# Attention with top-k, then GELU and two matrix products: PSUM banks that hold two sums are opened by their first real product, without a product of zeros

## The chip, the cores and the metric

The kernel runs on one core of a Trainium2 chip. A core has five engines with a program each: TensorE (PE) multiplies matrices, VectorE (DVE), ScalarE (ACT) and GpSimd (POOL) work element by element, SyncE (SP) issues DMA transfers. The engines run side by side and wait for each other by semaphores. TensorE writes its results to PSUM, a memory of 8 banks of 128 partitions by 512 numbers (float32), and other engines copy them from there to SBUF, the large memory on the core. The metric is the time of one execution on the device in microseconds (us), the median of several runs.

## The reference

```python
# q, k, v: 8 batches x 8 heads x 576 rows x 64
scores = scale * np.matmul(q, k.transpose(0, 1, 3, 2))
kth = np.partition(scores, -32, axis=-1)[..., -32:-31]
scores = np.where(scores >= kth, scores, -1000000000.0)
scores = scores - np.max(scores, axis=-1, keepdims=True)
attn = np.exp(scores)
attn = attn / (np.sum(attn, axis=-1, keepdims=True) + 1e-09)
x = np.matmul(attn, v)        # heads side by side: 4608 rows x 512
h = x @ w_in                  # 512 x 2048
g = 0.5 * h * (1.0 + erf(h * inv_sqrt2))
out = g @ w_out               # 2048 x 512
```

Everything is float32. In each row of scores the 32 largest are kept, the rest is left out of the softmax.

## The kernel before, in words

**Slots.** The order of the work on all engines is written out by hand. The main loop at the end of the kernel goes through the items of attention, 144 of them, each 128 query rows of a pair of heads. One pass of the loop is a slot, of 10 to 12 us. In slot `n` TensorE computes the scores of item n+2 (`scores`, L341 and L357, s_ps, and `last_keys`, L303, the last 64 keys), VectorE finds the 32 largest of each row of item n (`top_k`: MAX8 on L378, MATCH_REPLACE8 on L381, four and three times for each of two heads), ScalarE makes the softmax of item n-1 (`softmax`, L417 and L418), GpSimd scales it (`normalise`, L431) with reciprocals by VectorE (`inverse`, L404), TensorE transposes the weights of item n-2 (`transposes`, L455, L458, L481) and multiplies those of item n-3 with v (`attend`, L538 and L549).

**The two products behind attention** are cut into pieces that `mlp` sets between these steps, on TensorE's queue. The rows of x are taken in 20 ranges: 16 of 256 rows and 4 of 128. A `first_block` has the pieces of x @ w_in (`l1_piece`, L594, into h_ps); ScalarE's GELU (L610) makes g of it; a `second_block` has the pieces of g @ w_out. A range of 256 rows has four first and four second blocks, each for four of the 16 slices of 128 along the 2048 columns of g.

The second product has three forms:

- `full_piece` (L689), the very first range: one product of 512 columns after another into a bank.
- `even_piece` (L707, L710), the four ranges of 128 rows: even and odd slices are summed in the two halves of one bank, `acc[0]`; the other 256 columns in one half of a second bank, `acc[1]`.
- `seven_piece` and `trio_piece`, through `products` (L743, L745), the 15 other ranges: two by two blocks are multiplied with seven products in place of eight. The sums and differences of w_out (`weight_sums`) and of g (`sums`, L625 to L628) are made by GpSimd. Product 7 goes to a bank `seven` and from there to SBUF at once (L761, L764). The six others are paired into three banks, `TRIO = ((1, 2), (6, 5), (4, 3))`: each bank holds two sums of 256 columns, one a half, which grow over the four blocks of the range. At the end ScalarE copies them out (L786 to L803) and GpSimd puts them together (L795 to L810). For the last range VectorE does that (`last_parts`, L827 to L837).

**Banks.** The accumulating banks have the tags y0, y1 and y2, one buffer each. From a few slots after the weights are in, all other small results of TensorE take turns on one bank with the tag z (`bank`: t_ps, tp_t, o, tp_qk, seven), so that each waits until the one before has been copied out.

**How a bank with two sums is opened.** A product with `start=True` overwrites its place, one with `start=False` adds to it. `acc_tile` gives the tile of a bank, and with `open_bank` it first issues a product of zeros over all 512 columns (L668), flagged as the start. Its operands are read again and again from a single column `none` of zeros in bfloat16. All real products into the bank are then issued with `start=False`. Banks that take one sum (L689, L710, `seven`) are flagged on their first real product. `trio_piece` calls `acc_tile` in the first block of a range, for each of its three banks just ahead of the first product into it: the first bank follows `seven`, with the transposes of the slot (L303, L455 or L458, then eight of L481) between the first bank's products and those of the other two. `even_piece` calls it for the first slice.

Of the kernel before, what the change touches and what calls it, by code (L numbers as in the profile page):

```python
# [14 lines left out]
def kernel(  # L15
# [19 lines left out]
    nc = tc.nc  # L35
    f32, i32, u32 = mybir.dt.float32, mybir.dt.int32, mybir.dt.uint32
    bf16, i16, u16 = mybir.dt.bfloat16, mybir.dt.int16, mybir.dt.uint16
# [4 lines left out]
    P = 128  # L42
# [9 lines left out]
    FT = DFF // P  # L52
# [3 lines left out]
    HALF = DM // 2  # L56
# [5 lines left out]
    const = ctx.enter_context(tc.tile_pool(name="const", bufs=1))  # L62
    work = ctx.enter_context(tc.tile_pool(name="work", bufs=2))
    ps = ctx.enter_context(tc.tile_pool(name="ps", bufs=2, space=bass.MemoryType.PSUM))
# [506 lines left out]
    g_of, acc, h_of = {}, {}, {}  # L571
# [5 lines left out]
    B1, B2 = slice(0, HALF), slice(HALF, DM)  # L577
# [65 lines left out]
    def store(tok, y):  # L643

        lo = 0
        while lo < P:
            two, at = divmod(tok + lo, RING)
            b, row, end = (
                (0, at, SM + TL) if at < SM + TL
                else (1, at - TL, SM + 2 * TL) if at < SM + 2 * TL  # L650
                else (1, at - SM - 2 * TL, RING)
            )
            m = min(end - at, P - lo)
            row += (2 * two + b) * S
            nc.sync.dma_start(out=out[row : row + m, :], in_=y[lo : lo + m])
            lo += m

    none = const.tile([P, 1], bf16, name="none")
    nc.gpsimd.memset(none, 0.0)

    def zeros(n):
        return bass.AP(tensor=none.tensor, offset=none.offset, ap=[list(none.ap[0]), [0, n]])

    def acc_tile(x, open_bank=True):

        t = ps.tile([P, 2, HALF], f32, tag=f"y{x}", bufs=1, name="y_ps")
        if open_bank:
            nc.tensor.matmul(  # L668
                t.rearrange("p a n -> p (a n)"), lhsT=zeros(P), rhs=zeros(2 * HALF),
                start=True, stop=False,  # L670
            )
        return t

    def y_tile():
        return work.tile([P, DM], f32, tag="y", name="y")

    def part_tile():
        return work.tile([P, HALF], f32, tag="part", bufs=3, name="part")

    def full_piece(u, x):  # L680

        tok, n, f0, nf = units[u]
        i, sub = divmod(x, 2)
        f = f0 + i
        assert NWI + f // 2 in made
        if f == 0:
            acc[sub] = acc_tile(sub, False)
        g = g_of[u - u % 2][:, u % 2].rearrange("p (f n) -> p f n", f=nf)
        nc.tensor.matmul(  # L689
            acc[sub].rearrange("p a n -> p (a n)"), lhsT=g[:, i, sub * P : (sub + 1) * P],  # L690
            rhs=w_out_sb[:, f, :], start=(f == 0), stop=(f == FT - 1),
        )
        if f == FT - 1:
            y = y_tile()
            nc.scalar.copy(out=y, in_=acc.pop(sub).rearrange("p a n -> p (a n)"))
            store(tok + sub * P, y)

    def even_piece(u, f_at):

        tok, n, f0, nf = units[u]  # L700
        f = f0 + f_at
        assert f // 2 in summed
        if f == 0:
            acc[0], acc[1] = acc_tile(0), acc_tile(1, False)
        lhsT = g_of[u - u % 2][:, u % 2].rearrange("p (f n) -> p f n", f=nf)[:, f_at]
        w = w_out_sb[:, f]
        nc.tensor.matmul(  # L707
            acc[0][:, f % 2], lhsT=lhsT, rhs=w[:, B1], start=False, stop=(f == FT - 1)
        )
        nc.tensor.matmul(  # L710
            acc[1][:, 0], lhsT=lhsT, rhs=w[:, B2], start=(f == 0), stop=(f == FT - 1)
        )
        if f == FT - 1:
            y, e = y_tile(), part_tile()
            nc.scalar.copy(out=e, in_=acc[0][:, 0])
            nc.scalar.copy(out=y[:, B1], in_=acc[0][:, 1])
            nc.scalar.copy(out=y[:, B2], in_=acc[1][:, 0])

            def end():
                nc.gpsimd.tensor_tensor(y[:, B1], y[:, B1], e, op=ALU.add)  # L720
                nc.gpsimd.tensor_tensor(y[:, B2], y[:, B2], e, op=ALU.add)
                store(tok, y)

            small.append((2, end))

    def products(u, names, x):

        _, _, f0, _ = units[u + x]
        j = f0 // 2
        assert j in summed and NWI + j in made  # L730
        g = g_of[u][:, x].rearrange("p (f n) -> p f n", f=2)
        t = sums_of[u][:, x]
        e, o, w = w_out_sb[:, f0], w_out_sb[:, f0 + 1], w_sum[:, j]
        lo, hi = slice(0, P), slice(P, 2 * P)
        sides = {
            1: (g[:, 0, lo], e[:, B1]), 2: (g[:, 1, lo], o[:, B1]), 3: (t[:, 2], o[:, B2]),
            4: (g[:, 1, hi], w[:, 2]), 5: (t[:, 0], e[:, B2]), 6: (t[:, 1], w[:, 0]),
            7: (g[:, 0, hi], w[:, 1]),
        }
        for k, name in enumerate(names):  # L740
            lhsT, rhs = sides[name]
            if name == 7:
                nc.tensor.matmul(seven[0][:, 0:HALF], lhsT=lhsT, rhs=rhs, start=(x == 0), stop=(x == 1))  # L743
                continue
            nc.tensor.matmul(  # L745
                acc[names][:, k], lhsT=lhsT, rhs=rhs,
                start=False, stop=(j == FT // 2 - 1 and k == 1),
            )

    seven, small = [None], []  # L750
# [3 lines left out]
    def seven_piece(u):  # L754
        j = units[u][2] // 2
        seven[0] = bank("seven")
        for x in range(2):
            products(u, (7,), x)
        if j == 0:
            y7[0] = work.tile([P, HALF], f32, tag="y7", bufs=2, name="y7")  # L760
            nc.scalar.copy(out=y7[0], in_=seven[0][:, 0:HALF])  # L761
            return
        t = work.tile([P, HALF], f32, tag="p7", bufs=1, name="p7")
        nc.scalar.copy(out=t, in_=seven[0][:, 0:HALF])  # L764
        into = y7[0]
        small.insert(0, (1, lambda: nc.gpsimd.tensor_tensor(into, into, t, op=ALU.add)))
# [3 lines left out]
    def trio_piece(u, names, x):  # L770
        tok, _, f0, _ = units[u + x]
        j, k = f0 // 2, TRIO.index(names)
        if j == 0:
            acc[names] = acc_tile(k)
        products(u, names, x)
        if j < FT // 2 - 1:
            return
# [169 lines left out]
    for pair in range(2, n_pairs):  # L947
        b, p = divmod(pair, NP)
# [131 lines left out]
```

## Time and profile before

| | before |
|---|---|
| median of 3 runs | 1619.91 us (1619.59 to 1622.13) |
| the profiled execution | 1620.02 us |
| its span, first to last instruction | 1618.2 us |
| mean granted clock of TensorE | 0.997 |
| VectorE busy, 0 to 134 us | 126.4 us |
| TensorE / VectorE busy, 230 to 620 us | 385.7 / 357.2 us |
| TensorE / VectorE busy, 1530 to 1618 us | 81.6 / 7.2 us |
| bytes moved by DMA | 56.31 MB, 35 GB/s |

The profile is of one execution. PE stands for TensorE's products and PEld for the loads of their weights, which run beside the product before. A float32 product is two passes, with a row each for load and product; a bfloat16 product or a transpose is one pass. The end of a product is modelled and covers its whole passage, so that rows of consecutive products overlap: what a product costs is read from the start of one to the start of the next. The time of a row is counted from the span's start. In a row of the timeline, a bracket tells how long the engine was idle before it, and what ended that. The chain of waits is followed back from the last instruction, at each step to what released it or to the instruction before it on its engine; "issue" is time for which the profile shows no reason.

### The profile page before, as it was taken

The numbers are of one execution on the slowest core, as the hardware profiler recorded it, in microseconds if no ns is written. First come the engines' busy times: TensorE is split into PE (matmuls) and PEld (weight loads), VectorE is DVE, ScalarE is ACT, GpSimd is POOL, SyncE is SP. The second block draws the span as 40 slices with busy tenths as digits, with TensorE's granted clock in tenths as the row PEclk, the third lists the DMA queues.
The fourth block names the chain that finished last, engine by engine and source line by source line (L and its number), as shares of the span: only waits on it lengthen the run. The fifth ranks groups of instructions, "written<-read, shape, count | busy, mean of one in ns | idle before, by whom it ended". The sixth has DMA issues, their size and how long they took to land.

```text
span 1618.2 us, 27709 instructions
## 1 busy us (share of the span) xinstructions
PE 1578.8 (98%) x10062; PEld 1269.9 (78%) x10081; DVE 1415.7 (87%) x3052; ACT 1205.9 (75%) x2122; POOL 772.9 (48%) x1045
## 2 busy tenths in 40 slices
PE   7899999999999999999999999999999999999998
PEld 6776678888787778888787778888878777888887
DVE  8999989989999889998999898998999988999800
ACT  6989877777778777777777777777777877776730
POOL 4775766433544445433454535443454444543442
PEclk9999999999999999999999999999999999999999
DMA  6523210011100110011110111001110011000000
GB/s 167 149 92 112 82 43 1 14 38 37 25 12 16 43 42 17 1 29 37 30 29 16 29 30 44 1 14 36 38 23 14 15 29 23 15 1 14 7 14 13
DMA packets 126920, 56.31 MB, mean 35 GB/s; under 512 B 117792, under 2 KB 118336, under 8 KB 126784
## 3 DMA queue, kind: packets, MB, share of 16 engines
q1 hardware_dynamic: 125520, 54.12, 12.5%
q8 instruction: 79, 1.29, 0.3%
q10 hardware_dynamic: 1200, 0.39, 0.1%
q14 instruction: 57, 0.47, 0.1%
q0 software_dynamic: 64, 0.03, 0.0%
HBM read 45.08 MB, written 9.44 MB: 34 GB/s over the span
## 4 chain that ended last, share of the span: by engine, by line
PE 90%; DVE 7%; ACT 2%; POOL 1%; issue 1%; DMA 0%; ACTq 0%; DVEq 0%; POOLq 0%
PE h_ps L594 31%; PE y_ps L745 19%; PE o L538 8%; PE s_ps L341 7%; PE tp L481 7%; DVE top L378 4%; DVE rest L381 3%; PE seven L743 3%; PE tp_qk L263 2%; PE tp_t L303 2%; PE y_ps L707 2%; PE y_ps L710 2%; PE y_ps L689 2%; PE s_ps L357 1%; PE tp_t L455 1%; PE o L549 1%
## 5 line engine op out<-in xcount | busy, mean ns | idle before, releaser
L378 DVE MAX8 top<-rest 128x8 f32<-128x576 f32 x864 | 609.9, 748 | 0.0
L594 PE MATMUL h_ps<-xT,w_in_sb 128*128 128x256 f32 (+1 forms) x2560 | 560.7, 363 | 1.0 <-ACT g L610 1.0
L594 PEld LDWEIGHTS h_ps<-xT,w_in_sb 128*128 128x128 f32 x2560 | 428.9, 191 | 82.5 <-issue 34.6
L381 DVE MATCH_REPLACE8 rest<-top,rest 128x576 f32<-128x576 f32 x576 | 423.7, 744 | 0.0
L410 POOL TENSOR_SCALAR den<-den 128x2 f32<-128x2 f32 x144 | 31.7, 220 | 671.3 <-ACT s L418 671.2
L431 POOL TENSOR_TENSOR s<-s,rden 128x1152 f32<-128x1152 f32 x139 | 292.8, 2106 | 0.3 <-DVE rden L404 0.3
L418 ACT ACTIVATE s<-s,bias 128x576 f32<-128x576 f32 x288 | 223.3, 775 | 12.8
L417 ACT ACTIVATE s<-s,neg 128x576 f32<-128x576 f32 x288 | 224.4, 779 | 0.1
L381 DVE MATCH_REPLACE8 rest<-top,s 128x576 f32<-128x576 f32 x288 | 211.8, 744 | 0.0
L497 ACT COPY pt<-tp 128x1024 f32<-128x1024 f32 x133 | 134.6, 1012 | 99.9 <-PE tp L481 99.6
L378 DVE MAX8 top<-s 128x8 f32<-128x576 f32 x288 | 201.9, 743 | 1.4 <-ACT s L347 1.4
L350 ACT ACTIVATE s<-s_ps 128x1024 f32<-128x1024 f32 x127 | 130.4, 1027 | 74.0 <-PE s_ps L341 61.9
L538 PE MATMUL o<-pt,raw_v 128*64 128x256 f32 x1280 | 154.9, 388 | 0.4 <-ACT pt L488 0.4
L481 PE MATMUL tp<-ident,s 128*128 128x128 f32 x1152 | 149.6, 273 | 0.0
L341 PE MATMUL s_ps<-kt,qm 64*128 64x256 f32 x1024 | 146.7, 405 | 0.8 <-ACT s L348 0.8
L481 PEld LDWEIGHTS tp<-ident,s 128*128 128x128 f32 x1152 | 134.5, 141 | 14.8 <-issue 2.1
L745 PE MATMUL y_ps<-w_out_sb,sum 128*128 128x256 f32 x480 | 142.8, 379 | 0.0
L538 PEld LDWEIGHTS o<-pt,raw_v 128*64 128x64 f32 x1280 | 87.4, 138 | 64.2 <-issue 20.3
L404 DVE RECIPROCAL rden<-den 128x2 f32<-128x2 f32 x144 | 22.8, 159 | 121.5 <-POOL den L410 121.5
L341 PEld LDWEIGHTS s_ps<-kt,qm 64*128 64x128 f32 x1024 | 88.8, 187 | 45.2 <-issue 27.8
L745 PE MATMUL y_ps<-w_out_sb,g 128*128 128x256 f32 x480 | 122.5, 379 | 0.8
L745 PEld LDWEIGHTS y_ps<-w_out_sb,sum 128*128 128x128 f32 x480 | 91.2, 190 | 12.4
(135 smaller groups left out, 2194.8 us busy)
## 6 DMA issues: line engine op xcount, KB each, us to landing
raw_q<-in_q_dram SPq DMA_DIRECT2D x64, 128.0 KB, 2.3
raw_v<-in_v_dram SPq DMA_DIRECT2D x64, 128.0 KB, 2.4
raw_k<-in_k_dram SPq DMA_DIRECT2D x62, 128.0 KB, 2.4
out_dram<-y SPq DMA_DIRECT2D x30, 256.0 KB, 2.1
w_out_sb<-in_moe_w_in_dram SPq DMA_DIRECT2D x14, 511.8 KB, 4.8
w_out_sb<-in_moe_w_out_dram SPq DMA_DIRECT2D x10, 511.8 KB, 4.4
w_sum<-in_moe_w_out_dram SPq DMA_DIRECT2D x6, 511.8 KB, 4.1
out_dram<-y SPq DMA_DIRECT2D x11, 128.0 KB, 2.3
```

Source lines behind the costliest of these rows:

```text
L341: nc.tensor.matmul(s_ps[:, e, c * 256 : (c + 1) * 256], lhsT=q_t[rows, :], rhs=kt[rows, 2 * P + c * 256 : 2 * P + (c + 1) * 256], start=Tr ...
L350: nc.scalar.activation(spread(s, S + TL, SM), s_ps, func=AF.Copy, scale=scale)
L378: nc.vector.max(st["top"][:, e, 8 * r : 8 * r + 8], cur[e])
L381: nc.vector.match_replace(rest[:, e], st["top"][:, e, 8 * r : 8 * r + 8], cur[e], LOWEST)
L417: nc.scalar.activation(s, s, func=AF.Prelu, bias=st["neg"][:, e, 1:2], scale=1.0, alpha=STEEP)
L418: nc.scalar.activation(s, s, func=AF.Exp, bias=st["bias"][:, e : e + 1], scale=1.0, accum_out=st["den"][:, e : e + 1],)
L431: nc.gpsimd.tensor_tensor(s, s, wide, op=ALU.mult)
L481: nc.tensor.transpose(tp[:, j * P : (j + 1) * P], s[:, first + j * P : first + (j + 1) * P], ident)
L497: nc.scalar.copy(out=pt_now[0][:, 0 : 2 * NM, x : x + P], in_=tp.rearrange("p e (j n) -> p (e j) n", j=NM),)
L538: nc.tensor.matmul(o[e * D : (e + 1) * D, 0:n], lhsT=vt[:, j, e, :], rhs=pt[:, e * NM + j if j < NM else 2 * NM, :], start=(j == 0), stop= ...
L594: nc.tensor.matmul(h_tile(u)[:, i, :], lhsT=w_in_sb[:, ko, f * P : (f + 1) * P], rhs=xT[:, ko, c0 : c0 + n], start=(ko == 0), stop=(ko == ...
L745: nc.tensor.matmul(acc[names][:, k], lhsT=lhsT, rhs=rhs, start=False, stop=(j == FT // 2 - 1 and k == 1),)
```

## The change

Three banks in a range of 256 rows, and one in a range of 128, lose their product of zeros. The first real product into such a bank is flagged in its place: for `trio_piece` that is the first product of the first block, into the half `k == 0`; for `even_piece` the first slice, into the first half. The first product into the other half is issued with `start=False`, as before. The tile `none` and its memset go.

```diff
-    none = const.tile([P, 1], bf16, name="none")
-    nc.gpsimd.memset(none, 0.0)
-
-    def zeros(n):
-        return bass.AP(tensor=none.tensor, offset=none.offset, ap=[list(none.ap[0]), [0, n]])
-
-    def acc_tile(x, open_bank=True):
-
-        t = ps.tile([P, 2, HALF], f32, tag=f"y{x}", bufs=1, name="y_ps")
-        if open_bank:
-            nc.tensor.matmul(
-                t.rearrange("p a n -> p (a n)"), lhsT=zeros(P), rhs=zeros(2 * HALF),
-                start=True, stop=False,
-            )
-        return t
+    def acc_tile(x):
+        return ps.tile([P, 2, HALF], f32, tag=f"y{x}", bufs=1, name="y_ps")
...
         if f == 0:
-            acc[0], acc[1] = acc_tile(0), acc_tile(1, False)
+            acc[0], acc[1] = acc_tile(0), acc_tile(1)
...
         nc.tensor.matmul(
-            acc[0][:, f % 2], lhsT=lhsT, rhs=w[:, B1], start=False, stop=(f == FT - 1)
+            acc[0][:, f % 2], lhsT=lhsT, rhs=w[:, B1], start=(f == 0), stop=(f == FT - 1)
         )
...
             nc.tensor.matmul(
                 acc[names][:, k], lhsT=lhsT, rhs=rhs,
-                start=False, stop=(j == FT // 2 - 1 and k == 1),
+                start=(j == 0 and k == 0), stop=(j == FT // 2 - 1 and k == 1),
             )
```

## The prediction

> **What bounds the kernel now.** I read the page's busy shares first, then its chain of waits, to learn which engine sets the end and whether its clock is held back.
>
> ```profile
> PE 1578.8 (98%) x10062; PEld 1269.9 (78%) x10081; DVE 1415.7 (87%) x3052; ACT 1205.9 (75%) x2122; POOL 772.9 (48%) x1045
> ...
> PEclk9999999999999999999999999999999999999999
> ...
> PE 90%; DVE 7%; ACT 2%; POOL 1%; issue 1%; DMA 0%; ACTq 0%; DVEq 0%; POOLq 0%
> ```
>
> TensorE is in 90% of the chain that ended last, with the clock granted in every slice. The busy times of the engines in stretches place the rest: DVE is busy 126.4 of the first 134.0 us, before the second product starts, and from 230 to 1464 us PE is busy 385.7 of 390, 375.8 of 380 and 459.7 of 464 us. So whatever is taken from TensorE's stream after 230 us should come off the end, unless another engine is waiting just behind it. DVE is the one to watch: 357.2 of 390, 347.2 of 380 and 427.1 of 464 us in the same stretches, 92%.
>
> Next, the instructions that write the tile y_ps, for the row that goes (columns: minimum/median/maximum ns, first and last start):
>
> ```profile
> L668 PEld LDWEIGHTS <-none x49: 97/98/100, 229.8 to 1577.3; 128*128 128x128 bf16 x49
> ...
> L668 PE MATMUL y_ps<-none x30: 379/379/380, 233.2 to 1577.5; 128*128 128x512 bf16 x30
> ```
>
> There are 49 weight loads but 30 matmul records: 45 openings by `trio_piece` (15 ranges of 256 tokens, three banks) and 4 by `even_piece`. The 19 records that lack are the first bank of each range and the four of `even_piece`; in the rows of the engine the next product starts late by one product there too, so all 49 run. 379 ns is a matmul's whole passage, with its modelled end; since matmuls overlap, it is not what one costs. The cost is the distance from one start to the next, and the chain in order of time shows that (start, length, what). First a slot that opens three banks, and then the next slot with a second block, where the same banks are continued:
>
> ```profile
> 229.29 0.86 PE seven L743 x4
> 230.15 0.05 issue
> 230.20 1.03 PE y_ps L745 x4
> 231.23 0.22 PE tp_t L303 x2
> 231.45 0.22 PE tp_t L458 x2
> 231.67 0.87 PE y_ps L745 x4
> 232.54 0.87 PE tp L481 x8
> 233.41 0.22 PE y_ps L668
> 233.62 1.73 PE y_ps L745 x8
> 235.35 0.21 PE y_ps L668
> 235.57 1.73 PE y_ps L745 x8
> ```
>
> ```profile
> 249.25 0.86 PE seven L743 x4
> 250.11 0.86 PE y_ps L745 x4
> 250.97 0.22 PE tp_t L303 x2
> 251.19 0.11 PE tp_t L455
> 251.30 0.87 PE y_ps L745 x4
> 252.17 0.87 PE tp L481 x8
> 253.04 3.46 PE y_ps L745 x16
> ```
>
> From `seven` to the last y_ps the first takes 8.01 us (229.29 to 237.30) and the second 7.25 us (249.25 to 256.50). The first transposes one tile more at the tail (L458 x2, 0.22, for L455, 0.11). What remains, 0.76 - 0.11 = 0.65 us, is three openings: 0.22 (the unrecorded one, inside "issue" and the 1.03 that is 0.86 elsewhere), 0.22 and 0.21. So one opening is 0.216 us of TensorE. The second slot is also what the first should look like after the change.
>
> **The change, part by part.** *The products of zeros go.* 49 x 0.216 = 10.6 us of TensorE's stream. Their weight loads (98 ns) lie beside the product before and cost nothing of their own. The memset of `none` (91 ns on POOL at 3.4 us, beside the first loads) is nothing; what hides it is the wait of 4.08 us for raw_k that leads the chain there.
>
> The Trainium skill, page "TensorE: Matmul & The Clock Gate", section "Back-to-back issue gap", speaks against so much: it gives about 131 ns as the sustained spacing of matmuls of 512 columns in a stream of loads and products, and some 216 ns only for an isolated one. By its 131 ns the openings would be an estimated 49 x 0.131 = 6.4 us; the chain's 0.22 and 0.21 stand in the middle of a stream, and I go by them.
>
> *The flag moves to a real product.* Its price is not in the old rows for this line, but the nearest row has the very form: L710 in `even_piece` opens half a bank with a flagged f32 product of 256 columns. In the timeline at 311.23 us its two passes are followed by the next product at 311.67, 0.44 us later, and the unflagged L707 at 311.67 is followed at 312.10, 0.43. Every fourth product of L594 is flagged as well, and 16 of its passes take 3.46 us in the chain, like 16 unflagged ones of L745. A gain from the flag is excluded, since it is the same product; the other end is a drain of the array, one whole passage (0.379 us) each, 18.6 us. I take 0, the row of the same form.
>
> *Waits.* The built program has the same waits and the same order on every engine, less the 49 pairs. One wait moves: the very last opening (product at 1577.48 us) waits for a ScalarE copy, and the first real product there takes that over; behind it on TensorE stand the remaining products of the last range. The copy is long done by then (the opening's load at 1577.26 us shows no idle time in front of it), so 0.
>
> *What the openings cover.* (a) The copy of `seven` (L761) runs while the first bank is opened, and L303 needs the same bank z after it. In the timeline L761 runs from 230.19 to 230.56 and L303's weight load starts at 230.85. Where L303 does wait for such a copy (398.49 + 0.37 = 398.86, load at 398.91) it starts 0.05 us behind. So the slack is 230.85 - 230.56 - 0.05 = 0.24 us, and 0.22 of it goes: 0.02 remain. Cost 0, but if the copy came 0.2 us later in the 14 such slots it would be 14 x 0.2 = 2.8 us. (b) In a slot with three openings DVE has little in hand: before its reciprocal at 610.72 us it idles 1.16 us and at 620.87 only 0.35, and the slot between would be 0.65 shorter. But PE computes scores two slots ahead and takes up weights two slots later, DVE idles 106.4 us in front of its reciprocals from 229 to 1505 us, and in those 1276 us PE's own list of waits names ACT alone and neither DVE nor POOL. So the shortfall is made up in the next slots: 0 here, and 0.65 - 0.35 = 0.30 in each of 14 slots, 4.2 us, if it is not. (c) At the end of attention it is not made up. The range opened at 1507 us is the last before DVE runs through: from its start at 1505.02 on it works without a break to
>
> ```profile
> 1524.50 0.17 DVE L404 RECIPROCAL rden<-den 128x2 f32<-128x2 f32 x1
> ```
>
> with no idle time in front, normalise (POOL L431) follows it, and PE waits for that at 1527.16 (L455, idle 0.45). PE arrives there 0.65 us earlier and waits that much longer: -0.65. The last range (1573 to 1577 us) has PE alone and counts in full, as the DVE end of L827 to L837 waits for PE.
>
> Sum: 10.6 - 0.65 = 9.9 us. The profiled execution took 1620.02 us with a span of 1618.2, so I expect 1610.1 and 1608.3; it stands 0.11 us over the median of the runs, 1619.91, which becomes 1610.0.
>
> **The rivals.** *DVE or ScalarE takes part of it* (end b, end a, or both): 9.9 - 4.2 = 5.7, 9.9 - 2.8 = 7.1, both 2.9 us, so 1612.8 to 1617.0. For it: 0.02 us left in (a), 0.35 against 0.65 in (b), DVE at 92%. Against: the list of waits, and the slots without openings, which have (a) just so and lose nothing visible.
>
> *The flag costs a drain* and ends on the other side: a flagged product that opens a shared bank holds TensorE until the products before it have passed, 49 x 0.379 = 18.6 us against 10.6, slower by 8.0: 1627.9. It decides from 10.6 / 49 = 0.216 us a flag. L710 and L594 speak against it.
>
> *The change does not do what it says*, that is, TensorE's time per slot is set by its sequencer or loads and the openings ran in time that is idle anyway: 1619.9. The two slots above, 0.65 apart, speak against it. What no run here shows, and what does not bear on the time: the Trainium skill, "PSUM — Partial Sum Buffer", section "The four PSUM rules", states that a flagged product clears the written-bits of its whole bank, so that the other half's first product overwrites.
>
> **How the numbers follow.** Forecast (10.6 or 9.9 us kept, 1609.3 to 1611): 0.79. DVE or ScalarE takes part: 0.14, most of it nearer to its small end. No effect: 0.04. Drain: 0.03. The runs of before differ by 2.5 us (1619.59 to 1622.13), and a measurement of this kernel tells some 0.2%, 3.2 us, from no change. The range goes from 1608.6, which is all 10.6 us (1609.3) and 0.7 of scatter, to 1613.6, which is (a) at 2.8 us (1612.8) and 0.8 of scatter; it leaves out (b) in full, no effect and the drain. Faster by over 0.2% means below 1616.7: forecast and nearly all of the first rival, 0.93; within 0.2%: 0.04; slower: 0.03.
>
> **What would show it.** In the profile after: no row of `none`; the slots that open banks run from `seven` to the last y_ps in 7.36 us (8.01 - 0.65); PE's instructions shrink by 30 recorded matmuls and 49 loads, the span by 9.9; L455 near 1517 us waits about 1.1 us for POOL instead of 0.45. Wrong would be L303 waiting for L761 in the opening slots (a), new waits of PE for POOL L431 before 1505 us or a reciprocal without idle time in front after each opening (b), or more than 0.43 us from a flagged y_ps product to the next.

## The result, and the profile after

| | before | after |
|---|---|---|
| median | 1619.7 us (6 runs, 1619.54 to 1622.13) | 1611.11 us (6 runs, 1609.49 to 1612.3) |
| ratio to before | | 0.9944, 95% interval 0.9931 to 0.9957 |
| the profiled execution | 1620.02 us | 1609.49 us |
| its span | 1618.2 us | 1607.7 us |
| from the first `seven` of the chain to the end of the span | 1618.2 - 229.29 = 1388.9 us | 1607.7 - 228.65 = 1379.1 us |

The change made the kernel faster by 8.6 us of median. The deletion shifts the code behind it: what stood on L743, L745, L761 and L764 is now on L730, L732, L748 and L751. The page's busy times and its chain, by engine:

```profile
PE 1568.1 (98%) x10032; PEld 1262.7 (79%) x10032; DVE 1415.5 (88%) x3052; ACT 1205.0 (75%) x2122; POOL 774.1 (48%) x1044
...
PE 89%; DVE 9%; ACT 2%; POOL 1%; issue 0%; DVEq 0%; POOLq 0%
```

TensorE loses 10.7 us of busy time in products and 7.2 in weight loads (49 of 0.098 us are 4.8 of these); no other engine changes by over 1.2 us. The share of VectorE in the chain goes from 7% to 9%; where that is will be seen below. The slot that opens three banks, in the chain in order of time (start, length, what):

```profile
228.65 0.86 PE seven L730 x4
229.52 0.86 PE y_ps L732 x4
230.38 0.22 PE tp_t L303 x2
230.60 0.22 PE tp_t L458 x2
230.82 0.87 PE y_ps L732 x4
231.68 0.87 PE tp L481 x8
232.56 3.46 PE y_ps L732 x16
```

It now runs as the slot that only continued the banks did before: 0.86 for the first four passes into y_ps, no "issue" between, and the other 16 passes in one piece of 3.46. From `seven` to the last product it is 7.37 us (228.65 to 236.02) in place of 8.01.

Where the time came from can be told to a hundredth, since the order of the real products is the same in both: the starts of the `seven` products, counted from the first one, show by how much the kernel before has fallen behind. It falls behind by 0.64 us in each range of 256 rows and by 0.21 in each range of 128, is 9.91 us behind at 1514 us (times of the changed kernel), gets 0.63 back by 1533, loses 0.65 in the last range and ends 9.92 behind. The first 229 us, in which no bank with two sums is opened, took 0.64 us less in this execution, in code that is the same but for the memset of `none`; that makes up the 10.5 us between the spans.

### The profile page after: what moved, and what is told of

It reads as the page before. It is cut to its first block, busy times and chain, and to the rows that moved or that the text cites. A ratio compares the mean times of both kernels' runs of the same rounds, so it can differ in the third digit from the quotient of the medians.

```text
span 1607.7 us, 27629 instructions
## 1 busy us (share of the span) xinstructions
PE 1568.1 (98%) x10032; PEld 1262.7 (79%) x10032; DVE 1415.5 (88%) x3052; ACT 1205.0 (75%) x2122; POOL 774.1 (48%) x1044
## 4 chain that ended last, share of the span: by engine, by line
PE 89%; DVE 9%; ACT 2%; POOL 1%; issue 0%; DVEq 0%; POOLq 0%
PE h_ps L594 31%; PE y_ps L732 19%; PE o L538 8%; PE s_ps L341 7%; PE tp L481 7%; DVE top L378 5%; DVE rest L381 4%; PE seven L730 3%; PE tp_qk L263 2%; PE tp_t L303 2%; PE y_ps L694 2%; PE y_ps L697 2%; PE y_ps L676 2%; PE s_ps L357 1%; PE o L549 1%; PE tp_t L455 1%
## 5 line engine op out<-in xcount | busy, mean ns | idle before, releaser
L410 POOL TENSOR_SCALAR den<-den 128x2 f32<-128x2 f32 x144 | 32.0, 222 | 656.3 <-ACT s L418 656.2
L431 POOL TENSOR_TENSOR s<-s,rden 128x1152 f32<-128x1152 f32 x139 | 293.0, 2108 | 0.3 <-DVE rden L404 0.3
L481 PE MATMUL tp<-ident,s 128*128 128x128 f32 x1152 | 149.6, 273 | 0.0
L481 PEld LDWEIGHTS tp<-ident,s 128*128 128x128 f32 x1152 | 134.6, 141 | 14.8 <-issue 2.1
L732 PE MATMUL y_ps<-w_out_sb,sum 128*128 128x256 f32 x480 | 142.8, 379 | 0.0
L732 PE MATMUL y_ps<-w_out_sb,g 128*128 128x256 f32 x480 | 122.5, 379 | 0.0
L732 PEld LDWEIGHTS y_ps<-w_out_sb,sum 128*128 128x128 f32 x480 | 91.2, 190 | 12.4
```

Of the source, the lines that this page charges most:

```text
L431: nc.gpsimd.tensor_tensor(s, s, wide, op=ALU.mult)
L481: nc.tensor.transpose(tp[:, j * P : (j + 1) * P], s[:, first + j * P : first + (j + 1) * P], ident)
L732: nc.tensor.matmul(acc[names][:, k], lhsT=lhsT, rhs=rhs, start=(j == 0 and k == 0), stop=(j == FT // 2 - 1 and k == 1),)
```

## Experiments

All are compared by the stretch from the first `seven` of the chain to the end of the span, 1388.9 us before and 1379.1 after, because it leaves out the scatter of the start. e4 to e7 are one execution each, so that their reading rests on the trace alone.

**Zeros for the first bank alone (e1).**

```diff
...
-                start=False, stop=(j == FT // 2 - 1 and k == 1),
+                start=(j == 0 and k == 0 and names != TRIO[0]), stop=(j == FT // 2 - 1 and k == 1),
...
-            acc[names] = acc_tile(k)
+            acc[names] = acc_tile(k, k == 0)
```

What is left out at the first mark is `even_piece`, whose bank is opened by the flag.

> The product of zeros is kept for the first bank of each of the 15 ranges alone; the two other banks and those of even_piece are opened by the flag. Theory (each opening is 0.216 us of TensorE's stream, and only the range opened last before DVE runs through gives nothing): from the first seven to the end of the span 14 x 0.216 = 3.0 us more than with no opening, 1379.1 + 3.0 = 1382.1 us against 1388.9 before; L748's copy is covered by 0.24 us again. Rival (ScalarE's copy of seven comes too late without the opening, so that this bank's opening was free in the 14 slots): 1379.1 to 1379.3. Rival (the gain is scatter of the start and not of the openings): no order by the number of openings.

Measured: 1610.9 - 228.81 = 1382.1 us, 3.0 over the changed kernel, and a median of 1612.89 us (ratio to before 0.996, interval 0.9948 to 0.9972). So 14 of these 15 openings were paid for in full (the starts of `seven` show the last one before the end of attention given back, as expected), and taking them away costs no wait for the copy of `seven`: in the changed kernel's chain above L303 follows at once, though only 0.02 us of cover was reckoned to be left.

**Two products of zeros for each bank (e2).**

```diff
-            nc.tensor.matmul(
-                t.rearrange("p a n -> p (a n)"), lhsT=zeros(P), rhs=zeros(2 * HALF),
-                start=True, stop=False,
-            )
+            for x in range(2):
+                nc.tensor.matmul(
+                    t.rearrange("p a n -> p (a n)"), lhsT=zeros(P), rhs=zeros(2 * HALF),
+                    start=True, stop=(x == 0),
+                )
```

> Two products of zeros, one after the other, open each bank. Theory: 46 x 0.216 = 9.9 us more than before, and at the end of attention 0.65 us of which 0.45 is hidden in the wait of PE for POOL: from the first seven to the end 1388.9 + 9.9 + 0.2 = 1399.0 us, and the median 1619.7 + 10.1 = 1629.8. Rival (the openings ran in time that TensorE could spare, and what was gained came from elsewhere): 1388.9 and 1619.7.

Measured: 1628.4 - 228.87 = 1399.5 us, 10.6 more than before, and a median of 1630.29 us (ratio 1.0059, 1.0044 to 1.0074). The price of an opening holds on the other side too. But all 49 count here: I had expected 0.45 us of the 0.65 at the end of attention to vanish in the wait of L455, and that wait still is 0.44 us (the row of the timeline at 1536.70 us). A wait is no reserve when what ends it hangs on the waiting engine itself: the chain of before goes from PE's transposes (L481 at 1520.66) by ScalarE's copy and softmax to POOL L431 and back to PE. When PE comes later, POOL does too. These are lines of that chain (start, length, what), and then three rows of the timeline before:

```profile
1520.66 0.89 PE tp L481 x8
1521.57 1.01 ACT pt L497
1522.59 0.68 ACT s L417
1523.29 0.88 ACT s L418 x2
...
1525.05 2.07 POOL s L431
```

```profile
1523.04 1.41 DVE L378 MAX8 top<-rest 128x8 f32<-128x576 f32 x2
...
1524.25 0.22 POOL L410 TENSOR_SCALAR den<-den 128x2 f32<-128x2 f32 x1 [3.99 <-ACT s L418]
...
1527.16 0.33 PE L455 MATMUL tp_t<-ident,s 128*128 128x128 f32 x1 [0.45 <-POOL s L431]
```

VectorE's last MAX8 of the item ends at 1524.45 us, and POOL L410, which follows ScalarE, at 1524.47: two paths to POOL L431, through VectorE and through PE and ScalarE, end within 0.02 us of each other.

**A narrow product of zeros ahead of the flagged one (e3).**

```diff
-                t.rearrange("p a n -> p (a n)"), lhsT=zeros(P), rhs=zeros(2 * HALF),
-                start=True, stop=False,
+                t[:, 0, 0:64], lhsT=zeros(P), rhs=zeros(64), start=True, stop=True,
```

and the flags as in the changed kernel.

> Opened by the flag as in the changed kernel, with a product of zeros of 64 columns, a group of its own, ahead of each flagged product. Theory (an opening costs the stream of its columns, 512 in 0.216 us): 46 x 0.027 = 1.2 us over the changed kernel, from the first seven to the end 1380.3 us. Rival (the weight load of 98 ns is what it costs, once the stream is shorter): 46 x 0.098 = 4.5, 1383.6. Rival (a fixed price for an instruction of another type): 9.9, 1388.9.

Measured: 1614.0 - 229.88 = 1384.1 us, 5.05 over the changed kernel, 5.05 / 46 = 0.110 us each; median 1617.42 us (ratio 0.9974, 0.9964 to 0.9984). The theory of mine, that the columns are the price (1.2 us), falls for a narrow product; the rival of the weight load (4.5 us) is the nearest. Its chain in the same slot:

```profile
230.74 0.03 PE y_ps L668
230.77 0.95 PE y_ps L744 x4
...
233.02 0.87 PE tp L481 x8
233.89 0.03 PE y_ps L668
233.92 1.81 PE y_ps L744 x8
```

The product of zeros takes its 0.03 us, but the real ones after it take 0.95 for 0.86 and 1.81 for 1.73: 0.08 to 0.09 us are lost behind it. A weight load runs beside the product before; a load of 0.19 us (the rows of y_ps) does not fit beside a product of 0.03. That this is the cause is argued from the rows and not tried by itself, and it gives no size: 0.19 less 0.03 would be 0.16. The Trainium skill, page "TensorE: Matmul & The Clock Gate", section "LDWEIGHTS (loading the stationary operand)", puts a load at its columns divided by 1.2, so 107 ns for 128 columns; 46 of these would be an estimated 4.9 us, near the 5.05 measured, though the row of the zeros' own load says 98 ns.

**All products flagged (e4).**

```diff
-            acc[0][:, f % 2], lhsT=lhsT, rhs=w[:, B1], start=(f == 0), stop=(f == FT - 1)
+            acc[0][:, f % 2], lhsT=lhsT, rhs=w[:, B1], start=True, stop=True
...
-                start=(j == 0 and k == 0), stop=(j == FT // 2 - 1 and k == 1),
+                start=True, stop=True,
```

> Every product into the two-sum banks is flagged as a start, 735 more flags than in the changed kernel; the sums of the second product are not made in it. Theory (a flag costs nothing): from the first seven to the end 1379.1 us, as the changed kernel. Rival (a flag holds TensorE until the products before it have passed): 735 x 0.379 = 279 us more.

Measured: 1610.4 - 229.79 = 1380.6 us, 1.6 more than the changed kernel, not 279. And the 1.6 are not the flags': in the chain 16 flagged passes into y_ps take the same 3.46 us, and up to the `seven` products that stand at 1589 us in the changed kernel the two run within 0.02 us of each other, counted from the first `seven`. What comes then, in the busy times by stretches (length, the busy time of PE, PEld, DVE, ACT and POOL, the granted clock):

```profile
114.00:1598.00 1484.00, 1465.47 (x9275) 1177.56 (x9274) 1306.19 (x2810) 1106.83 (x1961) 696.47 (x972) 1.00 0.10 27
1598.30:1601.70 3.40, 3.23 (x8) 2.61 (x9) 0.00 (x0) 0.37 (x1) 1.41 (x3) 0.50 0.00 0
1601.70:1608.00 6.30, 4.65 (x22) 3.76 (x20) 2.69 (x7) 0.37 (x1) 0.11 (x1) 1.00 0.12 42
```

For 3.4 us the clock is granted at half, just after the 2.43 us in which TensorE waits for POOL's last sums. That, and not the flags, is the 1.6: e6 below has such a stretch at the same place, with the few flags of the changed kernel. So a flag is free.

**Zeros in one range alone (e5, e6).** The condition on `tok` is the range's first row, 4096 in e5 and 4352 in e6.

```diff
...
-                start=False, stop=(j == FT // 2 - 1 and k == 1),
+                start=(j == 0 and k == 0 and tok != 4096), stop=(j == FT // 2 - 1 and k == 1),
...
-            acc[names] = acc_tile(k)
+            acc[names] = acc_tile(k, tok == 4096)
```

What is left out at the first mark is `even_piece`, opened by the flag, and the line that reads `tok`.

> Zeros open the three banks of one range alone, the last one that is opened while attention runs (rows 4096 to 4351); all other banks are opened by the flag. Theory (at the end of attention VectorE sets when TensorE goes on, so that these three openings cost nothing): from the first seven to the end 1379.1 us as in the changed kernel, and L455 waits about 0.45 us for POOL in place of 1.08. Rival (every opening costs the end its 0.216 us): 1379.7, L455 as in the changed kernel.

> Zeros open the three banks of the last range alone (rows 4352 on), where attention is over. Theory: TensorE alone sets the end there, 3 x 0.216 = 0.65 us more than in the changed kernel, from the first seven to the end 1379.7 us. Rival (the end hangs on the sums of POOL, for which TensorE waits 2.4 us): 1379.1, and that wait is 1.8.

Measured in e5: 1608.2 - 229.15 = 1379.05 us, and at the `seven` of 1589 us 0.01 over the changed kernel. Three openings for nothing. The waiting row of the timeline, first of e5 and then of e6:

```profile
1517.76 0.33 PE L455 MATMUL tp_t<-ident,s 128*128 128x128 f32 x1 [0.45 <-POOL s L431]
```

```profile
1517.36 0.33 PE L455 MATMUL tp_t<-ident,s 128*128 128x128 f32 x1 [1.07 <-POOL s L431]
...
1599.07 3.44 PE L745 MATMUL y_ps<-w_out_sb,g 128*128 128x256 f32 x8
```

The wait is 0.45 us with the openings and 1.07 without: they only move into it. In e6 the three openings of the last range cost 0.64 us at the `seven` of 1589 us, as the theory has it, and the wait for POOL at the end stays at 2.4 us. The whole stretch of e6 is 1610.1 - 228.76 = 1381.3 us, 1.6 more than expected, again because of a stretch of 3.4 us at a granted clock of 0.51, from 1599.2 us: eight passes take 3.44 us there, and 1.89 in the changed kernel.

**One real product less in each block (e7).**

```diff
             lhsT, rhs = sides[name]
+            if name == 3 and x == 1:
+                continue
...
-                start=(j == 0 and k == 0), stop=(j == FT // 2 - 1 and k == 1),
+                start=(j == 0 and k == 0), stop=(j == FT // 2 - 1 and k == (names != TRIO[2])),
```

> Product 3 of each second half of a block is left out (60 real products of 0.433 us, 26.0 us of TensorE), so the output lacks them: four times the openings, taken from every block. Theory (TensorE sets the time of the slots, and the other engines follow with room to spare): from the first seven to the end 1379.1 - 26.0 = 1353.1 us, less some 0.4 at the end of attention, 1353.5, and no new wait of TensorE. Rival (VectorE, busy 92% and with 96.7 us of idle time left in 1270, takes part): 1355 to 1360, with TensorE waiting for POOL or ScalarE where it did not before.

Measured: 1583.4 - 229.07 = 1354.3 us, 24.7 of the 26.0 gone. Counted at the `seven` products 22.3 of 22.9 are kept up to 1514 us of the changed kernel, another 0.42 is lost by 1533, at the known place, and the rest by the end. PE's list of waits from 228 to 1440 us names ScalarE alone, with 12.3 us in all, for 11.9 in the changed kernel over the same slots, up to 1462 us. So VectorE, which is busy 94% of e7 from 230 to 1460 us, shows no part in what is lost up to there, though 26.0 us are taken out in place of 10.6. They are taken in other portions: 0.43 us in each of the four slots of a range, where the change takes 0.65 in one. For that one slot the changed kernel itself is the test: it keeps 0.64 us in every range of 256 rows up to 1514 us. Together they refute this rival for the change.

**Both waits at the end filled (e8).**

```diff
-        t = work.tile([P, 2, 3, P], f32, tag="sum", bufs=1, name="sum")
+        if u == NU - 2:
+            r = work.tile([P, 2, S], f32, tag="rest", bufs=1, name="rest")
+            t = r.rearrange("p a n -> p (a n)")[:, 0 : 6 * P].rearrange("p (a x n) -> p a x n", a=2, x=3)
+        else:
+            t = work.tile([P, 2, 3, P], f32, tag="sum", bufs=1, name="sum")
...
+        if n == N - 1:
+            mlp(1)
         for x, piece in enumerate(now):
```

> The changed kernel with two edits at the end: one piece of products more ahead of the transposes in the slot where L455 waits 1.08 us for POOL, and the sums of the last block in the tile rest, which is free by then, so that POOL need not wait for TensorE's last reading of the sums before, and TensorE not 2.44 us for POOL. Theory: 0.86 (the piece fills the wait, and VectorE's end moves nothing) + 2.4 = 3.3 us less, from the first seven to the end 1375.8 us; and with no idle time of TensorE there, no stretch at half clock near the end, where the run with all flags had one of 3.4 us. Rival (ScalarE's chain behind the transposes comes later by the piece and takes it back): 1376.6.

Measured: 1604.4 - 228.78 = 1375.6 us, 3.4 less than the changed kernel, and a median of 1606.34 us (ratio to before 0.9911, 0.9895 to 0.9928): faster than both, as its slowest run is 3 us under the fastest of the changed kernel's six. In its timeline the piece fills most of the wait of L455, and the last `seven` follows the products before it without a wait:

```profile
1517.37 0.33 PE L455 MATMUL tp_t<-ident,s 128*128 128x128 f32 x1 [0.21 <-POOL s L431]
...
1593.75 0.59 PE L736 MATMUL y_ps<-w_out_sb,sum 128*128 128x256 f32 x2
1594.18 1.03 PE L734 MATMUL seven<-w_sum,g 128*128 128x256 f32 x4
```

0.71 us come from the piece of products and 2.7 from the sums' tile, read at the starts of `seven`, where 0.86 and 2.4 were expected: the sum is nearer than its parts, which miss on opposite sides. Its four runs lie within 0.3 us (1606.19 to 1606.47).

## Why the prediction was right

*The price of an opening, 0.216 us, with all 49 in the stream.* Right: 9.92 us from the first `seven` to the end where 9.9 were reckoned, 3.0 for 14 (e1), 10.6 more for 49 more (e2), 0.64 for three (e6). The distance of starts in the chain was the row to read; the 379 ns of the product's own row would have given 18.6 us. The 131 ns that the Trainium skill, page "TensorE: Matmul & The Clock Gate", section "Back-to-back issue gap", gives for a product of 512 columns in a stream, an estimated 6.4 us, do not hold in these runs: the products of zeros measured 0.216 us each.

*The flag at no cost.* Right: 735 more flags in e4 move TensorE by 0.02 us up to 1590 us. The drain, the rival on the other side, is refuted.

*Cover (a) and VectorE (b), both at no cost.* Right by e1, by the 0.64 us kept in each range of 256 rows up to 1514 us, by e7 with its larger sum, and by PE's list of waits from 228 to 1500 us, which is line for line that of before.

*The loss (c) of 0.65 us at the end of attention.* Right, 0.63, and e5 shows it by itself. PE's list of waits from 1490 us on in the changed kernel, and its chain there, in which VectorE now stands where PE, ScalarE and GpSimd stood before (lines under e2):

```profile
PE tp_t L455 <- POOL s L431: 1.3, 2, 1.1
```

```profile
1511.76 1.46 DVE rest L381 x2
1513.22 1.33 DVE top L378 x2
1514.55 0.07 DVE rden L404
...
1515.14 2.07 POOL s L431
...
1517.25 0.33 PE tp_t L455
```

The chain follows VectorE without a break from its reciprocal at 1495.04 to 1514.62 us, 19.6 us or 1.2% of the span; that is the step from 7% to 9%. What the prediction did not see is that before stood at a tie, with PE's own chain as late as VectorE's to 0.02 us; so less work on PE gained nothing there, and more of it (e2) cost everything.

*The median.* 1611.11 for 1610.0 forecast. The span of the profiled execution, 1607.7 for 1608.3, is the lower by the 0.64 us of its first 229 us. The forecast did not contain them, and they are scatter: the first `seven` stands at 228.65 to 229.88 us in the ten traces. Three of the six runs lie at 1609.49 to 1610.04, as reckoned, and three at 1612.18 to 1612.3; before, five lie at 1619.54 to 1619.91 and one at 1622.13. The term that was too small is the scatter, 0.7 to 0.8 us in the range's working, and 2.6 in the runs before and 2.8 after. e4 is in TensorE's order and durations the changed kernel and took 1612.13 us; its trace has 1.1 us more at the start and 1.6 at the end, both beside stretches of half clock that lie elsewhere or are missing in the changed kernel's trace. That the three upper runs had the same is likely by their granted clock (0.994 and 0.995, for 0.995 and 0.996) but not shown, as they left no trace.

## What to carry to other kernels

Price an instruction on a pipelined engine by the distance of starts around it, best by two stretches of the same trace that differ by it alone; then look for the one place where another engine is late by as much, because there the gain turns into a longer wait. A bank that holds two sums can be opened by the flag of its first real product at no cost; in the changed kernel this one flag serves both halves, since the first product into the other half has `start=False` and yet begins its sum anew. A product of zeros in its place is not cheap, even when narrow: 0.216 us with 512 columns, 0.110 with 64. A wait counts as reserve only if what ends it does not come from the waiting engine.

## What the runs showed of the hardware

An idle time of TensorE of 2.43 us, in a stream that is otherwise dense, was followed by 3.4 us at half clock in e4 and e6, and an idle time of 2.44 us at the same place in the changed kernel was not; the half clock cost some 1.6 us. The traces tell more of when: the clock's changes stand 3.41 us or a multiple of it apart (in e4 at 1598.26, 1601.67 and 1608.50 us), on a grid that lies differently in every execution. Of the idle time, 2.22 us in e4 and 2.27 in e6 fall into one step of this grid, and the half clock begins with the next. In the six other traces with an idle time of 2.43 to 2.44 us here (before, the changed kernel, e1, e2, e3 and e5) a border of the grid parts it, at most 1.8 us fall into one step, and no half clock follows. So what decided, it seems, was where the idle time lay; this is read from eight traces and was not tried by itself. The Trainium skill, page "TensorE: Matmul & The Clock Gate", section "What's actually happening", gives an idle window of about 3.4 us as what throttles the clock, and says that the windows run freely: the length of the stretches, 3.4 us, agrees, and the idle time here is shorter than a window. In e8, without this idle time, no stretch of half clock lies near the end before TensorE's last product.
